# Attention and expert layers on one core: first two attention steps on one side of PSUM, shared steps moved, weight rows loaded a job sooner, warm-up on a cleared tile

## The chip, the cores and the metric

The kernel runs on one core of a Trainium2 chip. The metric is the device time of one execution in microseconds; the median of several runs counts. The engines are named as in the profile: PE is TensorE's matmuls and PEld its weight loads, DVE is VectorE, ACT is ScalarE, POOL is GpSimd, and SP is SyncE, whose queue (SPq) issues nearly all DMA transfers.

## What is computed

An attention with a bias that a small network computes from positions, and on its output a pair of expert matrices with a rational activation between them:

```python
# q, k, v: (4, 8, 576, 64); w1 (1, 32), b1 (32), w2 (32, 8)
scores = q @ k.transpose(0, 1, 3, 2) / sqrt(64)
rel = pos[:, None] - pos[None, :]
x = log1p(abs(rel)) / log1p(maximum(pos[:, None], 1.0))
bias = relu(x[..., None] @ w1 + b1) @ w2          # (576, 576, 8)
attn = softmax(scores + bias.transpose(2, 0, 1))
x = (attn @ v)  -> (2304, 512)
h = x @ w_in                                      # (512, 2048)
g = (a0 + a1*h + a2*h*h + a3*h*h*h) / (1 + abs(b0)*abs(h) + abs(b1)*h*h + 1e-6)
out = g @ w_out                                   # (2048, 512)
```

The weights are split into a high and a low part for the expert matmuls (w_in and w_out arrive in a wider type than the engines work in).

## The kernel before

Three stages follow one another.

**The bias table** (to about 48 us). x depends on the row only by a factor, so the network is evaluated by rows of positions: 36 groups of 16 rows, in the order of the list `order` (groups are counted by their place y in it). For each group four relus go into a ring of 18 slots, on VectorE (line 734) or ScalarE (732); 24 matmul instructions a group (line 761, four column groups of 32) make 128x591 values in two banks of PSUM; ScalarE copies them out into `e` (767); a DMA writes `e` into the table in DRAM (`tab`, line 772); and `load_bias` (260) reads the chunks of the bias back (`bias<-tab`) as they become complete, chunks 3 and 4 of the first pair of heads behind the last group. Ahead of it, nine matmuls (713) on the identity `ident`, which POOL makes, keep TensorE busy for warm-up, and VectorE scales the positions `lts` in two pieces (709). `start(0)` and `start(1)`, which issue the scores and the score reductions of attention steps 0 and 1, stand behind groups y = 33 and 35.

**The attention** (to about 258 us). A unit is a pair of heads, a group two units; a unit's 576 rows are four steps of 128 rows and 64 rows left over. The left-over rows of a group's two units go together in one shared step, `(u, 4)` in the list `steps`; it stands after step `(u, 3)`, so a group has nine steps. Two steps i = 2r and 2r + 1 make a round, `rnd(r)`, r = 1 to 35. A shared step is the first of a round in rounds 3, 11, 20 and 29 and the second in rounds 6, 15, 24 and 33. Each round, in the order of the code: output copies of earlier steps (493), scores of both steps on PE (341) woven together, reduction of scores and bias on VectorE (`e_ttr`, 357), transposes (425) with ScalarE's copies `pt` (440), tails (452), the product with v (484), exponentials on ScalarE (373). `side(i)` says in which four of PSUM's eight banks step i works. `loads`, `done_to` and `load_rb` place the loads of q, k and v, the normalization of a finished unit's output (`e_norm`, line 408, POOL, but VectorE for unit 12 = `NX` and the last unit) and the way of its reciprocals through DRAM (`rs`, 462, and `rb`, 392 and 396) at steps of a group. The list `late` holds unit 12's norm.

Between them `job_plan(r)` lays the preparation of the expert weights: one job for each block, three rounds for two jobs. A job loads raw rows (`wx`, line 140), splits them (VectorE 156 and 181, POOL 177 and 188, ScalarE 165) and stores the high and low part (`ws`, line 128). `out(c)` stores the low part of job c and issues the load of a later job's rows; after round 2 the first loads go out.

**The expert layers** (to the end): lines 316 and 909 on PE, the activation on the others.

Of the kernel before, what the change touches and what calls it, by code (L numbers as in the profile page):

```python
# [9 lines left out]
F32 = mybir.dt.float32  # L10
F32R = mybir.dt.float32r
U32 = mybir.dt.uint32
AF = mybir.ActivationFunctionType
ALU = mybir.AluOpType
# [3 lines left out]
P = 128  # L18
B, H, S, D = 4, 8, 576, 64
# [5 lines left out]
NG = S // NROW  # L25
TW = 2 * S
EW = S + NROW - 1
# [10 lines left out]
def tile_attn_moe(  # L38
# [12 lines left out]
    V, A, G, T = nc.vector, nc.scalar, nc.gpsimd, nc.tensor  # L51
# [4 lines left out]
    ident = cpool.tile([P, P], F32, tag="ident", name="ident")  # L56
# [39 lines left out]
    WF = W.rearrange("p a s -> p (a s)")  # L96
# [136 lines left out]
    with tc.manual_schedule():  # L233
# [3 lines left out]
        with ExitStack() as actx:  # L237
# [68 lines left out]
            def mm1(s, j):  # L306
# [5 lines left out]
                for k in range(KD):  # L312
                    for z, (w, x) in enumerate(
# [4 lines left out]
                            start=(k == 0 and z == 0), stop=(k == KD - 1 and z == 2),  # L318
                        ), b + j)

            steps = [(0, 0), (0, 1), (0, 2), (1, 0), (1, 1), (0, 3), (0, 4), (1, 2), (1, 3)]
            for u in range(2, len(units), 2):
                steps += [(u, c) for c in range(5)] + [(u + 1, c) for c in range(4)]
            s2, prob, pt, tl, xs = {}, {}, {}, {}, {}
            rsum, rb = {}, {}

            def side(i):
                return 4 * ((max(i // 2, 1) - 1 + i) % 2)

            def e_qk(i):  # L330
                u, c = steps[i]
# [177 lines left out]

            def loads(i):  # L510
                g, c = divmod(i, UPG)
                for u, x, y in ((2 * g + 2, 0 if g else 4, 3 if g else 6), (2 * g + 3, 5 if g else 7, 8)):
                    if u < NU and c == x:
                        load_qk(u)
                    if u < NU and c == y and u != 3:
                        load_v(u)
                if i == UPG + 1:
                    load_v(3)
                p, r = divmod(i, 2 * UPG)
                r = {2: 0, 7: 1, 11: 2, 13: 3, 16: 4}.get(r)  # L520
                if r is not None and p + 1 < NP:
                    load_bias(p + 1, r)
                if i == NS - 18:
                    load_x(0, 0, 0, KD - 1)
                if i == NS - 5:
                    load_x(1, 1, 0, KD - 1)
# [3 lines left out]
            def done_to(k):  # L530
                g, c = divmod(k, UPG)
                u = 2 * g - 2
                if g > 0:
                    if c == (0 if g > 1 else 1) and u != NX or k == NS:
                        norms.extend(e_norm(u))
                    if c == 6 and g * 2 < NU:
                        norms.extend(e_norm(u + 1))
                    if c == 2 and u + 1 < NU - 1:
                        load_rb(u + 1)
                if k == NS - 8:  # L540
                    x12.append(xs[NX])
                    late.extend(e_norm(NX))
                if g < NU // 2 and c == (7 - g % 2 if g else 8):
                    load_rb(2 * g)

            def run(todo):
                while todo:
                    todo.pop(0)()
# [11 lines left out]
            def job_plan(r):  # L560
                q, ph = divmod(r - 4, 3)
                c = 2 * q
                plan = {k: [] for k in ("first", "act", "pool", "between", "pool2", "last")}
                if r < 4 or c >= len(jobs):
                    return plan
                a, b = jobs[c], jobs[c + 1]

                def hi(x):
                    return lambda: x[3][3](True, False)

                def out(c):
                    def go():
                        jobs[c][3][3](False, True)
                        run(list(after.get(c, [])))
                        if c + 3 < len(jobs):
                            jobs[c + 3][0]()
                    return go

                if ph == 0:
                    plan.update(first=a[1], act=a[2], pool=[a[4]], last=[a[3][0], hi(a)])  # L580
                elif ph == 1:
                    plan.update(
                        first=b[1], act=b[2], between=[a[3][1]], pool2=[a[3][2]],
                        last=[b[3][0], out(c), hi(b)],
                    )
                else:
                    plan.update(pool=[b[4]], between=[b[3][1]], pool2=[b[3][2]], last=[out(c + 1)])
                return plan

            def rnd(r):  # L590
                i = 2 * r
                plan = job_plan(r)
                loads(i)
                op = None
                while puts:
                    op = puts.pop(0)()
                for x in plan["first"]:
                    op = x()
                for x in plan["act"]:
                    x()  # L600
                us = ended(i - 4, i - 3)
                sa, sb = e_qk(i), e_qk(i + 1)
                b, o = side(i), side(i + 1)
                ZZ = (o + 1, o + 3)
                main, ends, adds, copy = e_tp(i - 2, (b, b + 1), ZZ, us)
                main_, ends_, _, copy_ = e_tp(i - 1, (b + 2, b + 3), ZZ)
                weave(sa[0] + sb[0], sa[1] + sb[1])
                for k in ("pool", "pool2"):
                    if not plan[k] and norms:
                        plan[k].append(norms.pop(0))  # L610
                        break
                for x in plan["pool"]:
                    x = x()
                    if op is not None:
                        behind(x, op)
                e_ttr(i, 0, True)
                op = e_ttr(i, 1)
                for x in plan["between"]:
                    op = x()
                for x in plan["pool2"]:  # L620
                    behind(x(), op)
                small = [ends[r] + ends_[r] + adds[r] for r in range(2)]
                weave(main[0][:4] + small[0] + main[0][4:] + main_[0], main[1] + small[1] + main_[1])
                copy(1, 2)
                copy(0, 1)
                copy_(0, 2)
                for j in range(2):
                    e_ttr(i + 1, j)
                put_tails(i - 2, 2, ZZ, us)
                put = e_pv(i - 3, b + 1) if i > 2 else None  # L630
                puts.append(e_pv(i - 2, b))
                hi = split_x(0, (i - NS + 12) // 2) if i in (NS - 12, NS - 10, NS - 8) else ()
                if i == NS - 4:
                    hi = split_x(0, KD - 1, x12[0][:, :TS[0]])
                for x in hi[:1]:
                    x()
                for k in (i, i + 1):
                    for j in range(2):
                        e_exp(k, j)
                recip(i - 2)  # L640
                recip(i - 1)
                if put:
                    put()
                for x in plan["last"] + list(hi[1:]):
                    x()
                done_to(i - 2)
                done_to(i - 1)
                run(late)
                loads(i + 1)
                if r == 2:  # L650
                    for x in jobs[:3]:
                        x[0]()

            def start(i):
# [33 lines left out]
            with ExitStack() as bctx:  # L688
# [6 lines left out]
                lts = tpool.tile([P, S], F32, tag="lts", name="lts")  # L695
                bts = tpool.tile([P, NG * 4], F32, tag="bts", name="bts")
                LCUT = 320
                nc.scalar.dma_start(out=cs, in_=cst)
                nc.sync.dma_start(out=lts[:, :LCUT], in_=ltab[:, :LCUT])
                nc.sync.dma_start(out=lts[:, LCUT:], in_=ltab[:, LCUT:])  # L700
# [4 lines left out]
                G.memset(wmin, -8.0 * 0x38000000)  # L705
                V.tensor_scalar(out=bts, in0=pts, scalar1=b1s, scalar2=None, op0=ALU.mult)
                A.activation(out=w28, in_=cs[:, 8 + 5 * NG:], func=AF.Identity, scale=8.0)
                for a, z in ((0, LCUT), (LCUT, S)):
                    V.tensor_scalar(
                        out=lts[:, a:z], in0=lts[:, a:z], scalar1=w1s, scalar2=None, op0=ALU.mult  # L710
                    )
                for x in range(9):
                    on(T.matmul(W[:, 6, 0:P], ident, ident, start=True, stop=True), 6)  # L713

                def dist(n):
                    return max(NROW * n + NROW, S - NROW * n)
# [25 lines left out]
                done = {16: 2, 19: 0, 26: 1}  # L742
                for n in order[:LEAD]:
                    relu(n)
                for y, n in enumerate(order):
                    if y == 13:
                        load_v(1)
# [1 line left out]
                        relu(order[y + LEAD])  # L749
                    i0 = NROW * n  # L750
                    mid = i0 + NROW - 1
                    pa = 2 * ((y if y >= NG - 2 else y + 2) % 4)
                    pa = (pa, pa + 1)
                    cuts = sorted({0, mid, 512, EW})
                    for a, z in zip(cuts, cuts[1:]):
# [8 lines left out]
                            ), b)  # L764
                    e = rpool.tile([P, EW], F32, tag="e", name=f"e{n}")
                    o = 512 * pa[0]
                    on(A.activation(  # L767
                        out=e, in_=WF[:, o:o + EW], func=AF.Identity, scale=rts[:, n:n + 1]
                    ), *pa)
                    g, k = divmod(n, 8)  # L770
                    x0 = S - NROW - i0
                    nc.sync.dma_start(
# [307 lines left out]
```

## Time and profile before

| what | value |
|---|---|
| median of 3 runs | 660.83 us (660.64 to 660.9) |
| the profiled execution | 662.25 us, its span 660.5 us |
| granted TensorE clock, mean | 0.999 |
| busy in the span: PE, DVE, ACT, POOL | 99%, 85%, 71%, 23% |
| share of the chain that ended last: PE, DMA, ACT | 96%, 1%, 1% |
| of it by line: 316, 909, 484, 341, 425, 761 | 30%, 30%, 12%, 11%, 6%, 6% |

The profile is one execution; durations are read there, in microseconds from the span's start. Matmuls are pipelined, so PE is busy 99% of the span though parts of it are slower than others: stretches have to be compared with like stretches. The chain that ended last is followed back from the end, and a row in it gives the start, the duration and the number of instructions. A round's length is read as the distance of the rows of line 341 that begin two rounds.

### The profile page before, as it was taken

To read this page: it belongs to the slowest core of one execution; us is meant where nothing else is said; L and a number is where in the kernel's file an instruction comes from. 1 tells how busy PE (TensorE), PEld (TensorE's weight loads), DVE (VectorE), ACT (ScalarE), POOL (GpSimd) and SP (SyncE) were. 2 spreads that over 40 slices of the span, in tenths; PEclk is the share of its full clock that TensorE was granted. 3 is DMA by queue.
4 is the path that set the end of the run, shared out by engine and by line. 5 is a ranking of instruction groups with operands and counts; after the bars stand their busy time and mean duration, and the time that the engine had idled before them with its cause. 6 is when DMAs were issued, how large, how long until landed. Compare 5 with 4: busy or idle time off the path is not lost.

```text
span 660.5 us, 16193 instructions
## 1 busy us (share of the span) xinstructions
PE 653.5 (99%) x6274; PEld 546.8 (83%) x6274; DVE 561.3 (85%) x1100; ACT 472.2 (71%) x758; POOL 154.1 (23%) x108
## 2 busy tenths in 40 slices
PE   9999999999999999999999999999999999999997
PEld 6657888888888878988888888989988888888996
DVE  7997889988988895899999989979769779687776
ACT  7988999999999987767667566576656555555551
POOL 0000233333433330122212121222221221212211
PEclk9999999999999999999999999999999999999999
DMA  7887878868987975452825607669431301312031
GB/s 242 294 310 226 273 240 266 259 228 231 321 277 226 330 238 167 156 187 72 264 97 164 229 21 249 214 207 318 146 111 49 129 0 65 110 42 86 1 113 48
DMA packets 74845, 118.98 MB, mean 180 GB/s; under 512 B 11904, under 2 KB 33808, under 8 KB 74768
## 3 DMA queue, kind: packets, MB, share of 16 engines
q1 hardware_dynamic: 74624, 117.79, 54.2%
q8 instruction: 49, 0.80, 0.5%
q14 instruction: 28, 0.23, 0.1%
q10 hardware_dynamic: 144, 0.16, 0.1%
HBM read 79.17 MB, written 35.61 MB: 174 GB/s over the span
## 4 chain that ended last, share of the span: by engine, by line
PE 96%; DMA 1%; ACT 1%; issue 1%; DVE 0%; SPq 0%; POOL 0%; DVEq 0%; ACTq 0%; POOLq 0%
PE ps L316 30%; PE ps L909 30%; PE ps L484 12%; PE ps L341 11%; PE ps L761 6%; PE ps L425 6%; DMA tab<-e 1%; DMA bias<-tab 1%; PE ps L713 1%; ACT pt L440 1%; ACT p L373 1%; DVE s L357 0%; SPq L260 0%; DVE pre L930 0%; ACT wh L165 0%
## 5 line engine op out<-in xcount | busy, mean ns | idle before, releaser
L879 POOL TENSOR_TENSOR gl<-m,r 128x1024 fp32r<-128x1024 f32 (+1 forms) x39 | 85.6, 2195 | 295.5 <-DVE m L872 255.7
L830 ACT ACTIVATE w<-ps,babs 128x1024 f32<-128x1024 f32 (+1 forms) x40 | 41.3, 1033 | 107.1 <-PE ps L316 103.4
L373 ACT ACTIVATE p<-s,m 128x576 f32<-128x576 f32 x144 | 110.5, 783 | 0.2 <-DVE m L357 0.2
L357 DVE CUSTOM_DVE_ANT_0 s<-ps,bias 128x576 f32<-128x576 f32 (+1 forms) x144 | 95.2, 682 | 10.1 <-PE ps L341 3.9
L440 ACT COPY pt<-ps 128x512 f32<-128x512 f32 (+1 forms) x109 | 71.9, 732 | 17.6 <-PE ps L425 17.0
L909 PE MATMUL ps<-wol,gh 128*128 128x512 f32 x216 | 84.2, 390 | 0.0
L909 PE MATMUL ps<-woh,gh 128*128 128x512 f32 x216 | 84.2, 390 | 0.0
L341 PE MATMUL ps<-k,q 64*128 64x288 f32 (+1 forms) x640 | 82.3, 418 | 0.4 <-ACT e L767 0.2
L842 DVE SCALAR_TENSOR_TENSOR u<-w,babs,ps 128x1024 f32<-128x1024 f32 (+1 forms) x40 | 46.9, 1172 | 38.1 <-ACT t L831 38.0
L484 PE MATMUL ps<-pt,v 128*64 128x128 f32 (+1 forms) x1280 | 78.2, 265 | 0.8 <-ACT pt L440 0.5
L484 PEld LDWEIGHTS ps<-pt,v 128*64 128x64 f32 x1280 | 65.1, 137 | 5.8 <-ACT pt L440 1.6
L316 PE MATMUL ps<-xb,wih 128*128 128x512 f32 (+1 forms) x240 | 68.8, 367 | 0.0
L341 PEld LDWEIGHTS ps<-k,q 64*128 64x128 f32 (+1 forms) x640 | 50.9, 175 | 20.8 <-issue 6.4
L837 ACT ACTIVATE u<-u 128x1024 f32<-128x1024 f32 (+1 forms) x40 | 39.1, 978 | 40.2 <-DVE u L842 40.0
L425 PEld LDWEIGHTS ps<-ident,p 64*128 64x128 f32 x1296 | 49.6, 138 | 8.7 <-DVE m L357 2.9
L858 DVE SCALAR_TENSOR_TENSOR gh<-t,cst,r 128x1024 fp32r<-128x1024 f32 (+1 forms) x40 | 47.0, 1174 | 9.3 <-ACT r L839 6.9
L909 PE MATMUL ps<-woh,gl 128*128 128x512 f32 x216 | 53.8, 389 | 0.0
L425 PE MATMUL ps<-ident,p 64*128 64x64 f32 x1296 | 51.8, 226 | 0.5 <-ACT p L373 0.2
L865 DVE SCALAR_TENSOR_TENSOR m<-u,qc,gh 128x1024 f32<-128x1024 f32 (+1 forms) x40 | 47.1, 1178 | 4.0
L316 PEld LDWEIGHTS ps<-xb,wih 128*128 128x128 f32 x240 | 44.5, 188 | 6.1
L872 DVE SCALAR_TENSOR_TENSOR m<-t,cst,m 128x1024 f32<-128x1024 f32 (+1 forms) x40 | 47.1, 1179 | 1.4
L851 DVE SCALAR_TENSOR_TENSOR t<-t,cst,ps 128x1024 f32<-128x1024 f32 (+1 forms) x40 | 47.0, 1175 | 1.4
(82 smaller groups left out, 1343.9 us busy)
## 6 DMA issues: line engine op xcount, KB each, us to landing
tab<-e SPq DMA_DIRECT2D x36, 295.5 KB, 3.5
wx<-in_w_in_dram SPq DMA_DIRECT2D x16, 512.0 KB, 5.4
wx<-in_w_out_dram SPq DMA_DIRECT2D x16, 512.0 KB, 4.2
v<-in_vp_dram SPq DMA_DIRECT2D x16, 320.0 KB, 6.3
ws<-wh SPq DMA_DIRECT2D x20, 256.0 KB, 4.7
ws<-wl SPq DMA_DIRECT2D x20, 256.0 KB, 4.3
q<-in_qt_dram SPq DMA_DIRECT2D x16, 288.0 KB, 4.1
k<-in_kt_dram SPq DMA_DIRECT2D x16, 288.0 KB, 3.3
```

Of the source, the lines that this page charges most:

```text
L316: on(T.matmul(hps[s][:, j, :w_], w[:, k, sl], x[:, k, :w_], start=(k == 0 and z == 0), stop=(k == KD - 1 and z == 2),), b + j)
L341: on(T.matmul(W[o, b, :SH], q[r, x], k[r, a * SH:(a + 1) * SH], start=True, stop=True), b)
L357: op = on(V.tensor_tensor_reduce(out=t3[:, a], in0=W[:, b:b + 2][:, a, :SH], in1=b3[:, a], scale=-0.125, scalar=least, op0=ALU.add, op1=AL ...
L373: A.activation(out=prob[i][:, z * S:z * S + S], in_=t, func=AF.Exp, bias=m, scale=-1.0, accum_out=sums[u % 4][:, k:k + 1],)
L425: on(T.transpose(W[:, b, o:o + 64], src[x, :], ident[x, x]), b)
L440: on(A.copy(out=t.rearrange("p x (r s) -> p r x s", r=2)[:, a:z], in_=W[:, to[a]:to[a] + z - a].rearrange("p r (x s) -> p r x s", s=64),), ...
L484: on(T.matmul(ps[y, o], vt[n][:, kc, y], w_, start=(kc == 0), stop=(kc == 4)), b, mem=(f"pt{i % 3}", f"tl{i // 2 % 2}"))
L851: on(V.scalar_tensor_tensor(out=rt[s, "t"], in0=rt[s, "t"], scalar=abs_[:, 1:2], in1=hp(s), op0=ALU.add, op1=ALU.mult,), *hb(s), mem="t")
L865: V.scalar_tensor_tensor(out=m, in0=rt[s, "u"], scalar=qc, in1=rt[s, "gh"].bitcast(F32), op0=ALU.add, op1=ALU.mult,)
L872: V.scalar_tensor_tensor(out=m, in0=rt[s, "t"], scalar=abs_[:, 0:1], in1=m, op0=ALU.add, op1=ALU.subtract)
L879: eng.tensor_tensor(out=lo, in0=rt[s, "m"], in1=rt[s, "r0"], op=ALU.mult)
L909: on(T.matmul(po[n, c], l[:, j, c * P:(c + 1) * P], r[fp][:, j, :], start=(first and x is a), stop=(last and x is z),), OB[c])
```

## The change

Five edits, all ahead of the expert layers:

1. `side` puts steps 0 and 1 both into banks 4 to 7 (before: 0 to 3 and 4 to 7); the table groups' banks shift by two groups, and the last group's `e` is made by VectorE instead of ScalarE.
2. `turned` holds groups 1 and 3: their shared step moves one place back, behind step `(u + 1, 0)`, so that it is the first of round 7 and 16. The loads of k, q and v for the next group, `load_rb` and the norms move to fit.
3. `out(c)` loads the rows of job c + 4 instead of c + 3, and ahead of the low part's store; four loads instead of three go out after round 2.
4. `run(late)`, the norm of unit 12, moves from the end of round 33 into round 34, behind the reductions of its first step.
5. The warm-up works on a tile `warm` that VectorE clears, with ten matmuls; the second piece of `lts` is scaled behind the relus of the first two groups.

```diff
+            turned = range(1, len(units) // 2 - 3, 2)
             steps = [(0, 0), (0, 1), (0, 2), (1, 0), (1, 1), (0, 3), (0, 4), (1, 2), (1, 3)]
             for u in range(2, len(units), 2):
-                steps += [(u, c) for c in range(5)] + [(u + 1, c) for c in range(4)]
+                if u // 2 in turned:
+                    steps += [(u, c) for c in range(4)] + [(u + 1, 0), (u, 4)]
+                    steps += [(u + 1, c) for c in range(1, 4)]
+                else:
+                    steps += [(u, c) for c in range(5)] + [(u + 1, c) for c in range(4)]
...
             def side(i):
-                return 4 * ((max(i // 2, 1) - 1 + i) % 2)
+                return 4 * ((i // 2 - 1 + i) % 2) if i > 1 else 4
...
-                for u, x, y in ((2 * g + 2, 0 if g else 4, 3 if g else 6), (2 * g + 3, 5 if g else 7, 8)):
+                for u, x, y in ((2 * g + 2, 0 if g else 4, 3 if g else 6), (2 * g + 3, 7 if g == 0 else 6 if g in turned else 5, 8)):
...
-                    if c == (0 if g > 1 else 1) and u != NX or k == NS:
+                    if c == (1 if g == 1 else 2 if g - 1 in turned else 0) and u != NX or k == NS:
                         norms.extend(e_norm(u))
...
-                if g < NU // 2 and c == (7 - g % 2 if g else 8):
+                if g < NU // 2 and c == (8 if g == 0 else 7 if g in turned else 7 - g % 2):
                     load_rb(2 * g)
...
                     def go():
+                        if c + 4 < len(jobs):
+                            jobs[c + 4][0]()
                         jobs[c][3][3](False, True)
                         run(list(after.get(c, [])))
-                        if c + 3 < len(jobs):
-                            jobs[c + 3][0]()
...
                 op = e_ttr(i, 1)
                 for x in plan["between"]:
                     op = x()
+                run(late)
...
-                run(late)
                 loads(i + 1)
                 if r == 2:
-                    for x in jobs[:3]:
+                    for x in jobs[:4]:
                         x[0]()
...
+                warm = tpool.tile([P, P], F32, tag="warm", name="warm")
+                V.memset(warm, 0.0)
...
-                for a, z in ((0, LCUT), (LCUT, S)):
+
+                def scale(a, z):
...
-                for x in range(9):
-                    on(T.matmul(W[:, 6, 0:P], ident, ident, start=True, stop=True), 6)
+                scale(0, LCUT)
+                for x in range(10):
+                    on(T.matmul(W[:, 6, 0:P], warm, warm, start=True, stop=True), 6)
...
                     relu(n)
+                scale(LCUT, S)
...
-                    pa = 2 * ((y if y >= NG - 2 else y + 2) % 4)
+                    pa = 2 * ((y + 2 if y >= NG - 2 else y) % 4)
...
-                    on(A.activation(
-                        out=e, in_=WF[:, o:o + EW], func=AF.Identity, scale=rts[:, n:n + 1]
-                    ), *pa)
+                    if y < NG - 1:
+                        on(A.activation(
+                            out=e, in_=WF[:, o:o + EW], func=AF.Identity, scale=rts[:, n:n + 1]
+                        ), *pa)
+                    else:
+                        on(V.tensor_scalar(
+                            out=e, in0=WF[:, o:o + EW], scalar1=rts[:, n:n + 1], scalar2=None, op0=ALU.mult
+                        ), *pa)
```

What the tables and positions do to the order on the engines is seen in three places. Line numbers of the changed kernel are some 5 to 16 higher; 341, 357, 408 and 425 become 346, 362, 413 and 430.

PE in rounds 6 and 7 (group 1), before: the shared step's scores (64x288, units 2 and 3 in turn) follow step `(2, 3)`'s in round 6.

```order
L341 MATMUL ps<-k_999,q_998 128x288 x4
L341 MATMUL ps<-k_999,q_998 64x288
L341 MATMUL ps<-k_1204,q_1203 64x288
...
L425 MATMUL ps<-ident,p_1431 128x64 x10
...
L484 MATMUL ps<-tl_1528,v_1102 64x128 x2
L341 MATMUL ps<-k_1204,q_1203 128x288 x8
```

PE in the same rounds now:

```order
L346 MATMUL ps<-k_1002,q_1001 128x288 x4
L346 MATMUL ps<-k_1209,q_1208 128x288 x4
L430 MATMUL ps<-ident,p_1436 128x64 x10
...
L489 MATMUL ps<-tl_1529,v_1107 64x128 x2
L346 MATMUL ps<-k_1002,q_1001 64x288
L346 MATMUL ps<-k_1209,q_1208 64x288
...
L346 MATMUL ps<-k_1209,q_1208 128x288 x4
```

The eight narrow matmuls have gone from the second step of round 6 to the first of round 7, and one step of unit 3 has come forward in their place.

SP's queue between rounds 26 and 28, before (ws are the stores of weight parts, wx the loads of raw rows, rs and rb the reciprocals):

```order
L462 DMA rs_3892<-rt_3891 10x128
L128 DMA ws_0_3807<-wl_0_3839 128x512
L140 DMA wx_1_3937<-in_w_out_dram 128x2048
L128 DMA ws_1_3939<-wh_1_3818 128x512
L392 DMA rb_3941<-rs_3892 64x512
```

and now, at the same place:

```order
L467 DMA rs_3897<-rt_3896 10x128
L140 DMA wx_0_3941<-in_w_in_dram 128x2048
L128 DMA ws_0_3812<-wl_0_3844 128x512
L128 DMA ws_1_3944<-wh_1_3823 128x512
L397 DMA rb_3946<-rs_3897 64x512
```

At one place in the queue the rows of the next block come, where those of this block came, and the store of the low part has gone behind them.

VectorE around the turn from round 33 to 34, before (L408 is the norm of unit 12, L493 the output copies, s_68 and s_69 the reductions of round 34):

```order
L493 COPY xs_4745<-ps 128x128
L408 TENSOR_TENSOR xs_4160<-xs_4160,rb_4532 128x576
L493 COPY xs_4745<-ps 128x128
L357 ISA s_68_0_4785,m_0_0_4786<-ps,bias_2985 128x288
...
L357 ISA m_1_0_4791 128x1
L357 ISA s_69_0_4832,m_0_0_4833<-ps,bias_2985 128x576
```

and now:

```order
L498 COPY xs_4748<-ps 128x128 x2
L362 ISA s_68_0_4786,m_0_0_4787<-ps,bias_2990 128x288
...
L362 ISA m_1_0_4792 128x1
L413 TENSOR_TENSOR xs_4165<-xs_4165,rb_4535 128x576
L362 ISA s_69_0_4835,m_0_0_4836<-ps,bias_2990 128x576
```

The norm has gone from between the two output copies to between the reductions of steps 68 and 69.

## Rows read from the trace of the kernel before

**Rows 1.** page's costly groups: line, engine, operation, count | busy, mean ns | idle

```profile
L909 PE MATMUL ps<-woh,gh 128*128 128x512 f32 x216 | 84.2, 390 | 0.0
```

**Rows 2.** windows, table stage: us, busy of PE, PEld, DVE, ACT, POOL; clock, DMA

```profile
7.67:46.55 38.88, 38.87 (x808) 25.54 (x804) 38.61 (x105) 36.58 (x62) 0.00 (x0) 1.00 0.81 287
```

**Rows 3.** timeline, start: start us, us, engine, line, operation, tiles, count, [idle before <-releaser]

```profile
0.81 0.20 POOL masks.py:197 MEMSET ident<- 128x128 f32 x1
...
1.43 4.21 PE L713 MATMUL ps<-ident 128*128 128x128 f32 x18 [1.43 <-POOL ident masks.py:199]
...
5.57 0.20 PEld L761 LDWEIGHTS ps<-ring,w 128*32 128x32 f32 x8 [0.22 <-ACT ring L732]
5.57 5.86 PE L761 MATMUL ps<-ring,w 128*32 128x271 f32 x112
6.03 0.20 PEld L761 LDWEIGHTS ps<-ring,w 128*32 128x32 f32 x4 [0.26 <-issue]
...
8.83 0.12 PEld L761 LDWEIGHTS ps<-ring,w 128*32 128x32 f32 x4 [0.30 <-issue]
...
9.25 1.32 PEld L761 LDWEIGHTS ps<-ring,w 128*32 128x32 f32 x44 [0.30 <-issue]
```

**Rows 4.** chain of waits, table to attention: start us, us, what, count

```profile
49.74 4.63 DMA tab<-e
55.42 4.37 DMA bias<-tab
...
62.24 2.30 PE ps L341 x24
```

**Rows 5.** waits, 46 to 62.2 us (total, times, longest), and step 1's reduction

```profile
DVE s L357 <- DMA bias<-tab: 1.5, 1, 1.5
...
50.01 0.76 DVE L357 CUSTOM_DVE_ANT_0 s<-ps,bias 128x576 f32<-128x576 f32 x1 [2.10 <-ACT p L373]
```

**Rows 6.** chain of waits, rounds of groups 1 to 4

```profile
79.79 2.30 PE ps L341 x24
...
103.30 2.14 PE ps L341 x16
...
109.10 2.30 PE ps L341 x24
...
114.97 2.14 PE ps L341 x16
...
126.65 2.14 PE ps L341 x16
...
132.44 2.30 PE ps L341 x24
...
179.28 2.14 PE ps L341 x16
```

**Rows 7.** chain of waits, then timeline: round 29

```profile
214.38 1.23 PE ps L341 x16
...
220.70 2.14 PE ps L341 x16
...
211.19 0.41 SPq L140 DMA_DIRECT2D wx<-in_w_out_dram  x1
...
215.38 0.43 DVE L156 TENSOR_SCALAR wk<-wx 128x512 uint32<-128x512 uint32 x1 [0.60 <-DMA wx<-in_w_out_dram]
```

**Rows 8.** chain of waits, timeline of VectorE, waits: rounds 33 and 34

```profile
244.40 0.73 PE ps L341 x4
...
250.54 2.14 PE ps L341 x16
...
240.93 0.69 DVE L181 SCALAR_TENSOR_TENSOR wm<-wm,wh 128x512 uint32<-128x512 uint32 x1
...
244.69 0.76 DVE L408 TENSOR_TENSOR xs<-xs,rb 128x576 f32<-128x576 f32 x1 [0.88 <-DMA rb<-rs]
...
PEld ps L341 <- DVE xs L493: 0.6, 1, 0.6
```

## The prediction, made before the changed kernel was run

> **What bounds the kernel now.** I read the list of costly groups first. The expert layers from 257.7 us on leave TensorE (PE) no idle time [rows 1], so no part of this change, all of which lies ahead of them, can be lost or won there: whatever the attention stage ends earlier shifts the rest of the kernel as a whole. What is to be found is the microseconds ahead of 257.7 us in which PE waits, and whether each of the five edits reaches one.
>
> The windows come next. In the bias-table stage VectorE (DVE) is all but as full as PE: 38.61 of the 38.88 us between 7.67 and 46.55 [rows 2]. A PE that starts sooner there has 0.27 us of DVE's idle time to win, and then meets DVE.
>
> The timeline of the start shows PE's slow stretch. The passes over 271 columns come 0.46 us apart (5.57, 6.03), which is 1.70 ns a column; group 0's passes over 497 columns (its piece from column 15 to 512) come 0.42 us apart (8.83, 9.25), 0.85 ns a column [rows 3]. [...] The passes between them put the rise at about 7.0 us, 5.6 us after the first warm-up matmul at 1.43; behind it the granted clock reads 1.00 [rows 2].
>
> The chain of waits between table and attention shows what sets the start of round 3 (a round is two attention steps, and starts with its scores on line 341): tab<-e, the last table rows going out (49.74, 4.63 us), bias<-tab, their reading back (55.42, 4.37 us), and then the scores at 62.24 [rows 4]. The waits of that stretch say that DVE's score reduction (L357) waits 1.5 us for the bias transfer [rows 5].
>
> Last, the chain through the attention gives each round's length as the distance of two score rows. A plain round is 5.80 us (103.30 to 109.10), one with a shared step in first place 5.87 (109.10 to 114.97) [rows 6]. Two rounds stand out: 214.38 to 220.70 is 6.32 us [rows 7], and 244.40 to 250.54 is 6.14 [rows 8].
>
> **The change, part by part.**
>
> *Warm-up on a cleared tile.* Before, it waits for ident on GpSimd (POOL), whose clearing starts at 0.81 and takes 0.20 us, and a second operation behind it; PE starts at 1.43 [rows 3]. The new tile needs one clearing of the same size, alone on DVE. If DVE begins at about 0.75 as the others do and takes POOL's 0.20, PE starts near 0.98, some 0.45 us sooner. The tenth matmul keeps the end where it was: nine take 4.21 us, ten 4.68, to 5.66, while the first table matmul stands at 5.57 behind the first relus [rows 3], and those still follow the first scaling. If the clock rises as long after the first warm-up as now, it rises 0.45 us sooner, and work done at twice the speed for 0.45 us gains half of that, 0.23. DVE's 0.27 allows it. The second scaling piece, moved behind the first relus, changes DVE's order and not its sum: 0. I take **−0.25**. The ends: 0, if the rise does not move; and −0.7, all that group 0 loses at the slow level (5.57 to 7.0 at half speed), if it rises before the table begins and ScalarE (ACT), which shares the relus, takes what DVE can't.
>
> *Steps 0 and 1 on one side of PSUM, the last eviction on DVE.* Step 1's scores no longer wait for the eviction of a table group but for DVE's reduction of step 0 in the same banks, and the last e stands on DVE between the two. Of the 2.10 us that DVE stands before step 1's reduction at 50.01 [rows 5], the eviction fills about 0.76 (as L408's 576 columns take, [rows 8]) and its wait for PE's last table group a little more; the other half, an estimated 1.0 us, is what rounds 1 and 2 may start sooner. But step 5, the second of round 2, needs a bias chunk that is complete only behind the last table group, and its way (tab out, bias back, 9.0 us of transfers) begins with the last e, which ends when PE's last table group ends, on either engine [rows 4]. So the 1.0 us goes into the wait of 1.5 us for that transfer [rows 5], which becomes 2.5: **0**. The bounds are −1.0, if that transfer comes sooner too, and +0.3, if the eviction ends later on DVE than on ACT by part of its 0.76 us.
>
> *Shared steps of groups 1 and 3 one step later.* A step shared by two units is dearer as the second of a round than as the first. Four rounds with it second, 79.79 to 103.30, take 23.51 us, the next four with it first, 103.30 to 126.65, 23.35: 0.16 less. Group 3's eight rounds, 132.44 to 179.28, take 46.84 as these eight take 46.86, so the same is taken for it [rows 6]. The change makes groups 1 and 3 like 2 and 4. The loads of q, k and v, the reciprocals' way back and two norms on POOL go with it, one step or a round later; POOL is idle most of that stage and the rows that they normalize are read only by the expert layers. **−0.30**; ends 0 (a transfer moved with it comes late) and −0.35.
>
> *Weight loads one job sooner.* Round 29's 0.45 us over a like round (6.32 against 5.87) has its cause in a DVE row: L156 waits 0.60 us for wx, ahead of everything that DVE owes PE in that round; its transfer was issued at 211.19, 3.6 us before it was wanted [rows 7]. With the change this load stands at the place of the one before it, a round earlier or more, so it has landed. Cost: in SP's queue the load now stands ahead of a low-part store, which starts later by one transfer; nothing reads that store for many rounds. One further load of 512 KB goes up front after round 2, where q, k, v and the next bias chunk follow it with several microseconds in hand. **−0.45**; ends 0 (another wait takes its place) and −0.60, DVE's whole wait.
>
> *The norm of unit 12 moved into round 34.* Before, DVE reaches it at the end of round 33 and stands 0.88 us for rb, then 0.76 us on the norm, and only then copies the output (L493) for which PE's weight load waits 0.6 us; that round is 6.14 against 5.80 [rows 8]. After, it stands behind the first step's reductions in round 34; by then rb, there at 244.69, has landed, and the place is where other rounds have the join of L181 (0.69 us) and stay at 5.80 [rows 8]. **−0.35**; ends 0, if DVE is late for step 69's reductions, and −0.40.
>
> *Sum:* −0.25 + 0 − 0.30 − 0.45 − 0.35 = −1.35 us. The profiled execution took 662.25 us, with a span of 660.5; the sum gives it 660.9 and a span of 659.15. The median of the three runs is 660.83, so **659.45** is the forecast, given as 659.4.
>
> **The rivals.**
>
> (a) *The clock rises where it did.* Nothing in the trace shows that the rise follows the first matmul; one rise is there to read. Then the start gives 0, and the time is 660.83 − 1.10 = 659.7. For it: a single reading can't tie the rise to the engine's start. Against: the three runs lie within 0.26 us, and a rise at a random moment would scatter them by up to half of its own scatter.
> [...]
>
> (b) *The start is not held by the bias transfer*, and rounds 1 and 2 bring their 1.0 us: 659.45 − 1.0 = 658.45. For it: the transfer tab<-e of 4.63 us [rows 4] shares the DMA engines with other loads, and may be shorter if those come sooner. Against: the last table rows end with PE, and with DVE full PE's end moves by 0.25 us at most.
>
> (c) *One of the three attention terms comes back*: the norm on DVE in round 34 only moves its 0.76 us in front of step 69, or a load moved with the shared steps is late. Losing one of 0.30 to 0.45, or two in part, gives about 660.0.
>
> (d) *Slower than before: the cleared tile doesn't raise the clock.* Then the rise comes as long after the first table matmul as now after the first warm-up, 5.57 + 5.57 = 11.1 instead of 7.0. Half of those 4.1 us is lost, 2.05, and PE and DVE being both full there, none of it comes back: 660.83 + 2.05 − 1.10 = 661.8. It decides against the change from a rise at 9.2 us on, where half of the delay eats the 1.10. Against it: the engine runs the same instructions on zeros as on ident, and ident is nearly all zeros too.
>
> **How the numbers follow.** Forecast 0.42, (a) 0.24, (b) 0.14, (c) 0.13, (d) 0.07. A measurement of this kernel can tell about 0.2% from no change, 1.32 us: faster is below 659.51, slower above 662.15. The forecast lies at that edge and splits, 0.24 faster and 0.18 same; (a) gives 0.06 and 0.18; (b) is faster; (c) same; (d) 0.02 same and 0.05 slower. That makes 0.44, 0.51 and 0.05. The range: below, 658.4 takes in (b); above, (c) with both small terms lost and no gain at the start ends at about 660.7. Outside are (d) and the tails of (b) and (c), some 0.2. The forecast's own range is 659.0 to 659.9.
>
> **What would show it.** First warm-up matmul near 1.0 us and the pass over 271 columns turning fast before 7.0 (start); L357's wait for bias<-tab growing from 1.5 to 2.5 us with round 3 at 61.9 to 62.1 (no gain by the banks), or staying at 1.5 with round 3 at 61 (b); four-round sums of 23.35 in groups 1 and 3; round 29 at 5.87 and no wait of L156 for wx; round 34 at 5.80 and L408 waiting for nothing. From round 3 to the first expert matmul it should be 1.10 us shorter. A first warm-up later than 1.43, or round 3 after 62.24, makes the start wrong; any round over 5.9 that was 5.8 makes (c) right.

## The result

The changed kernel is slower: 666.81 us against 660.87 for the kernel before, ratio 1.0081 (95% interval 1.0057 to 1.0104). Its six runs spread from 663.22 to 667.49 us, those of the kernel before from 660.51 to 661.89. The forecast was 659.4, with a range from 658.4 to 660.7. The loss is 0.8%, small, but clear of the noise.

The profiled execution took 667.49 us, its span is 665.7 (660.5 before). From the start of each round's scores the place of the loss is found: the changed kernel begins round 28 still 0.25 us ahead of the profile before, then round 28 takes 11.82 us instead of 5.80, and from there to the end it stays 5.2 to 5.8 behind. Here are the chain of waits of the changed kernel around that round (start us, us, what), the waits of ScalarE's and PE's from 204 to 216 us, the row of ScalarE that ends the wait, and the windows (busy us of PE, PEld, DVE, ACT, POOL; then granted clock, DMA share, GB/s):

```profile
207.69 6.58 DMA ws<-wh
...
215.62 4.53 PE ps L489 x40
220.15 2.58 PE ps L346 x24
...
223.90 2.40 PE ps L489 x40
```

```profile
ACT wh L165 <- DMA ws<-wh: 4.1, 1, 4.1
PEld ps L489 <- ACT pt L445: 4.0, 1, 4.0
PE ps L489 <- ACT pt L445: 3.9, 1, 3.9
```

```profile
214.37 0.72 ACT L165 ACTIVATE wh<-wk,wmin 128x512 uint32<-128x512 uint32 x1 [4.07 <-DMA ws<-wh]
```

```profile
206.00:211.50 5.50, 5.50 (x92) 4.85 (x94) 4.71 (x18) 4.30 (x10) 2.62 (x3) 1.00 0.92 256
211.50:215.60 4.10, 0.24 (x8) 0.10 (x4) 1.66 (x8) 1.23 (x3) 0.95 (x1) 0.79 0.76 236
215.60:222.73 7.13, 7.11 (x70) 5.87 (x72) 2.86 (x9) 5.11 (x11) 1.41 (x1) 0.64 0.92 292
222.73:230.00 7.27, 7.21 (x135) 6.30 (x132) 6.52 (x20) 5.96 (x13) 2.70 (x3) 1.00 1.03 381
```

Read from below: ScalarE's line 165 writes the high part `wh` of a weight block. `wh` has two buffers, and the one that it needs is still being stored (`ws<-wh`, issued at 207.69, landed at 214.27). ScalarE stands 4.07 us, and behind it on the same engine stands the copy `pt` (line 445) that PE's product (489) needs. PE is busy 0.24 of 4.10 us, and the granted clock falls to 0.64 as the mean of the next 7 us. The product that takes 2.40 us a round later takes 4.53; over just these 4.53 us the granted clock is 0.50. 3.9 us of waiting and 2.1 us of slow clock make up the 6.0 us of that round.

What answers to the rows of before, in the changed kernel (timeline of the start, waits of 46 to 62.2 us, chain):

```profile
1.05 4.63 PE L723 MATMUL ps<-warm 128*128 128x128 f32 x20 [1.05 <-DVE warm L704]
```

```profile
DVE s L362 <- DMA bias<-tab: 1.9, 1, 1.9
```

```profile
79.58 2.14 PE ps L346 x16
...
102.92 2.14 PE ps L346 x16
...
126.26 2.14 PE ps L346 x16
...
243.96 2.30 PE ps L346 x24
...
249.98 2.14 PE ps L346 x16
...
255.78 2.14 PE ps L346 x16
```

The warm-up starts 0.38 us sooner than in [rows 3]. The wait for the bias transfer grew from 1.5 to 1.9 us [rows 5]. The eight rounds of [rows 6] take 46.68 instead of 46.86, four and four 23.34, so that the first four are 0.17 shorter; the forecast had 0.15 for each group. Round 34 (249.98 to 255.78) takes 5.80 where [rows 8] had 6.14.

### The profile page after: what moved, and what is told of

Its sections match the earlier page's. It is cut to its first block, busy times and chain, and to the rows that moved or that the text cites. A ratio compares the mean times of both kernels' runs of the same rounds, so it can differ in the third digit from the quotient of the medians.

```text
span 665.7 us, 16206 instructions
## 1 busy us (share of the span) xinstructions
PE 655.0 (98%) x6276; PEld 550.2 (83%) x6276; DVE 561.9 (84%) x1102; ACT 470.6 (71%) x757; POOL 153.5 (23%) x108
## 4 chain that ended last, share of the span: by engine, by line
PE 91%; DMA 4%; ACT 2%; SPq 1%; DVE 1%; issue 1%; ACTq 0%; DVEq 0%
PE ps L316 30%; PE ps L925 30%; PE ps L489 11%; PE ps L346 9%; PE ps L772 6%; PE ps L430 5%; DMA ws<-wh 2%; DMA tab<-e 1%; SPq L260 1%; ACT pt L445 1%; DMA wx<-in_w_in_dram 1%; PE ps L723 1%; ACT p L378 1%; DVE s L362 0%; ACT wh L165 0%
## 5 line engine op out<-in xcount | busy, mean ns | idle before, releaser
L489 PE MATMUL ps<-pt,v 128*64 128x128 f32 (+1 forms) x1280 | 80.1, 269 | 5.1 <-ACT pt L445 4.6
L489 PEld LDWEIGHTS ps<-pt,v 128*64 128x64 f32 x1280 | 66.7, 139 | 10.1 <-ACT pt L445 6.6
```

Source lines behind the costliest of these rows:

```text
L489: on(T.matmul(ps[y, o], vt[n][:, kc, y], w_, start=(kc == 0), stop=(kc == 4)), b, mem=(f"pt{i % 3}", f"tl{i // 2 % 2}"))
```

## The experiments

Which part does it? Each run below is compared with the kernel before on the same chip; "ratio" is the ratio of times with its 95% interval.

**1. The changed kernel without the weight loads' edit.** Loads are again those of job c + 3, behind the low part's store, three up front.

> The changed kernel with the weight loads where they were before (job c+3, behind the low part's store, three up front). Theory W (the load ahead of the stores makes the store of a high part land late, and ScalarE's line 165 waits for it): the 4.07 us wait of round 27 goes, PE's clock doesn't fall, and the time is about 660.87 + 6.2 - 0.9 lower than the changed kernel's, 659.9 to 660.4 (round 29 keeps its 0.45). Theory T (the moved shared steps and norm stores make SP's queue late): the wait stays and the time is 664 to 667.

665.58 us, ratio 1.0061 (1.0041 to 1.0082). The waits of ScalarE from 60 to 258 us keep the row:

```profile
ACT wh L165 <- DMA ws<-wh: 2.4, 1, 2.4
```

My first suspicion, the load ahead of the stores (theory W), falls, and with it theory B of the next run, that it takes both edits.

**2. The changed kernel without the moved shared steps.**

> The changed kernel with the shared steps of groups 1 and 3, their loads and norms where they were before. Theory W: the wait of line 165 stays, 664 to 667. Theory T: the wait goes, 659.4 to 660.0. Theory B (it takes both, since each adds a microsecond or two to SP's queue and there was little slack): about 659.8 here and 660.2 without the weight loads' change.

660.57 us, ratio 0.9995 (0.9986 to 1.0004). ScalarE waits for no store. The slowness is gone; the gain that theory T hoped for (659.4 to 660.0) isn't there.

**3. The weight loads' edit alone.**

> The kernel before with only the weight loads a job sooner. Theory W: line 165 waits for a store of a high part by 2 us or more in rounds 25 to 28, 663 to 667. Theories T and B: no such wait over 0.5 us, 660.4 to 661.0.

661.18 us, ratio 1.0008 (0.9999 to 1.0016). Line 165 waits once, 0.7 us in round 29; the profile puts that down to VectorE and not to a store, and what it waited for isn't shown.

**4. The moved shared steps alone.**

> The kernel before with only the shared steps of groups 1 and 3 moved. Theory W and B: 660.87 - 0.3 = 660.5, no wait of line 165 over 0.5 us. Theory T: that wait, 663 to 667.

664.02 us, ratio 1.0046 (1.0027 to 1.0065); the profile has line 165 waiting for stores four times, 3.9 us in all. The shared steps are the cause, alone and in company. With them gone (2, 3) the loss is not there.

**Why.** SP's queue of the changed kernel (start us, us, operation) at the end of group 3, then that of the kernel before at the same place:

```profile
158.54 0.55 SPq L273 DMA_DIRECT2D v<-in_vp_dram  x1
159.14 0.49 SPq L266 DMA_DIRECT2D q<-in_qt_dram  x1
159.68 0.49 SPq L267 DMA_DIRECT2D k<-in_kt_dram  x1
160.27 0.31 SPq L467 DMA_DIRECT2D rs<-rt  x1
160.68 0.34 SPq L140 DMA_DIRECT2D wx<-in_w_out_dram  x1
164.96 0.46 SPq L397 DMA_DIRECT2D rb<-rs  x1
...
169.89 0.65 SPq L196 DMA_DIRECT2D wih<-wh  x1
```

```profile
155.88 0.31 SPq L462 DMA_DIRECT2D rs<-rt  x1
...
158.59 0.55 SPq L392 DMA_DIRECT2D rb<-rs  x1
...
167.04 0.65 SPq L196 DMA_DIRECT2D wih<-wh  x1
...
204.44 0.38 SPq L128 DMA_DIRECT2D ws<-wh  x1
```

and SP's wait in the changed kernel (155 to 167 us):

```profile
SPq L397 <- DMA rs<-rt: 3.9, 1, 3.9
```

With the shared step a round later, the unit's reciprocals (`rs`) are written a round later, but the loads of v, q and k stay, and so come ahead of it. `rb` reads `rs` back and must wait until it has landed: SP stands from 161.0 to 164.96, and everything that is queued behind it is late, the store of `wh` at 167.04 now at 169.89. The lateness shrinks (a store at 180.85 in the profile before goes out at 181.83) and grows again, but it doesn't go away: the store of 204.44 before is the one of 207.69 above. There the buffer had been free in time; now it wasn't. A stand of SP before a read-back is nothing new in itself: between 60 and 200 us the kernel before has five, of 2.4 to 5.0 us (one of them from 195.4 to 198.5), and no wait of line 165. The changed kernel has two besides, 3.6 us from 105.6 on and the 3.9 us above: those of the groups whose shared step was moved.

**5. The moved steps alone, with `rb` one round later still.**

```diff
+                if c == 0 and g - 1 in turned:
+                    load_rb(2 * g - 2)
...
-                if g < NU // 2 and c == (8 if g == 0 else 7 if g in turned else 7 - g % 2):
+                if g < NU // 2 and g not in turned and c == (8 if g == 0 else 7 - g % 2):
```

> The kernel before with the shared steps of groups 1 and 3 moved, and the way back of their reciprocals (rb) one round later still, so that SP reaches rb long after rs has landed. Theory Q (SP stands some 4 us before rb of unit 6, all stores of high parts behind it land late, and ScalarE's line 165 waits for them): no wait of line 165 over 0.5 us between 150 and 230 us, the moved steps' 0.3 us come through, 660.5 to 660.9 beside a before of 660.9 to 661.05. Theory N (the norm's store of unit 6, which has moved beside rs, does it): still 663 to 666.

661.27 us, ratio 0.9999 (0.9986 to 1.0012), no wait of line 165, and SP's two new stands are gone. Theory N falls: the norm's store of unit 6 stands where the change put it. The 0.3 us that the moved steps should bring aren't seen in the time, whose interval is 0.9 us to either side.

**6. The whole change with the edit of 5.**

> The changed kernel whole, with one edit: rb of groups 1 and 3 one round later. Theory Q (SP's stand before rb is what makes the whole change slow): no wait of line 165 over 0.5 us, PE at 2.40 us for every product of round 27 and 28, and 660.5 to 661.6, the time of before. Rival (the weight loads ahead of the stores make a wait of their own once SP is late): 662.5 or more.

661.52 us, ratio 0.9998 (0.9989 to 1.0007). Moving the read-backs of the two groups takes away the whole loss of 0.8%. Its chain at the rounds that were slow:

```profile
205.16 2.40 PE ps L489 x40
207.56 2.14 PE ps L346 x16
209.70 1.26 PE ps L430 x38
210.95 2.40 PE ps L489 x40
```

and its SP queue where the stand was; rs has 5.4 us to land, and the store of `wh` goes ahead of rb:

```profile
155.57 0.31 SPq L467 DMA_DIRECT2D rs<-rt  x1
...
160.30 0.65 SPq L196 DMA_DIRECT2D wih<-wh  x1
161.00 0.64 SPq L397 DMA_DIRECT2D rb<-rs  x1
...
199.83 0.38 SPq L128 DMA_DIRECT2D ws<-wh  x1
```

The last row is the store that went out at 207.69 in the changed kernel.

**7. The moved steps alone, rb where the change has it, but v, q and k behind it.**

> The kernel before with the shared steps of groups 1 and 3 moved as in the change, rb where the change has it, but the loads of v and of the next group's q and k (896 KB) that the change leaves ahead of rs in SP's queue put behind rb, as they stand before. Theory Q1 (rs lands late because those loads are ahead of it in the queues): SP's gap between rs and rb of unit 6 falls from 4.3 us to 3 or less, no wait of line 165 over 0.5 us, about the time of before, 660.5 to 661.3. Theory Q2 (rs itself, a round later, is too late, whatever stands ahead of it): waits of line 165 stay, 663 or more.

663.25 us, ratio 1.0042 (1.0017 to 1.0067). In the profiled execution (span 660.8) `rs` goes out at 157.09 instead of 162.01 in run 4, SP stands 2.7 us before `rb` (157.95 to 160.64; 3.6 in run 4, 0.1 in the kernel before), and line 165 waits only twice, 0.23 and 0.35 us. So the loads ahead of `rs` are a part of the lateness, but with a shorter stand most of the loss in time is still there (1.0042 against 1.0046 in run 4). Neither theory holds whole. The longest round of this profile is round 29 with 6.94 us, where VectorE's L156 waits 1.2 us for `wx`; what the other executions of this kernel waited for, no profile shows.

So the loss hangs on the place of the read-back (5, 6). It leaves why the other four edits, together (6) and in parts (2, 3), bring nothing, where the sum said 1.05 us without the shared steps; the intervals of runs 2 and 6 leave out these 1.05 and the 1.35 of the whole.

**8. The kernel before once more.**

> The kernel before once more, for a second profile. If the profile that the prediction rests on was ordinary, round 3 starts at 62.2 us, round 29 takes 6.33 and round 34 6.14 again. If those waits change from run to run, at least two of the three differ by 0.3 us or more.

661.16 us, ratio to the other runs of the same kernel 1.0007 (0.9997 to 1.0017). Its profiled execution took 660.81, its span 659.0, 1.5 less than the one that I had read. Chain, and VectorE's row for the weights in round 29:

```profile
61.56 2.30 PE ps L341 x24
...
213.70 2.30 PE ps L341 x24
...
219.57 2.18 PE ps L341 x16
...
243.26 2.26 PE ps L341 x16
...
249.11 2.14 PE ps L341 x16
```

```profile
214.01 0.42 DVE L156 TENSOR_SCALAR wk<-wx 128x512 uint32<-128x512 uint32 x1
```

Round 3 begins 0.68 us sooner than in [rows 4], round 29 takes 5.87 instead of 6.32 [rows 7] with no wait for wx, round 34 takes 5.85 instead of 6.14 [rows 8]. These three differences are 0.68 + 0.45 + 0.29 = 1.42 us: all but 0.1 of the distance between the two profiled executions of one kernel.

**9. The start alone (warm-up, one side, last eviction on VectorE).**

> The kernel before with the warm-up on the cleared tile, steps 0 and 1 on one side and the last eviction on VectorE. By the prediction -0.25, 660.7; if round 3 isn't held by the bias transfer -1.0 to -1.2, 659.8; by the first rounds of the traces so far (0.3 to 0.4 us sooner than in kernels without it) 660.5 to 660.7.

661.08 us, ratio 0.9995 (0.998 to 1.001).

**10. The start and the norm in round 34.**

> The kernel before with the start's edits and the norm of unit 12 in round 34 alone. If both terms were worth what one profile showed, -0.25 - 0.35: 660.3 to 660.6. If the start's gain is swallowed by the transfers that round 3 waits for and the norm's wait of the one profile was chance, the time of before, 660.8 to 661.2.

661.26 us, ratio 1.0007 (0.9993 to 1.0022). Both are the time of before. In these two profiles round 4 takes 7.62 and 9.79 us instead of 5.87: L156 waits 1.8 and 2.6 us for `wx`. In the changed kernel and in run 12 the same wait is 0.3 and 0.4 us, in most of the others it isn't there. Which of the two levels PE has at the first table passes of 271 columns is seen in the distance of the weight loads (PEld), here of run 10, whose warm-up begins at 1.05:

```profile
5.61 0.20 PEld L767 LDWEIGHTS ps<-ring,w 128*32 128x32 f32 x8 [0.23 <-ACT ring L737]
6.07 0.20 PEld L767 LDWEIGHTS ps<-ring,w 128*32 128x32 f32 x4 [0.26 <-issue]
```

0.46 us a pass, as in [rows 3], the slow level, though the warm-up began 0.38 us sooner; in the changed kernel the loads of two such passes stand at 5.88 and 6.10, 0.22 us apart. (The granted clock reads 1.00 from 0 to 5 us in the profiles of both kernels; the level is read from the distances alone.) In run 5, which keeps the warm-up of before (1.43), the same passes follow one another in one row of 2.33 us for 64 loads, at the fast level. Over the fourteen profiled executions the first of these passes is slow in five: three of seven with the old warm-up (both of the kernel before, and run 12) and two of seven with the new (1 and 10); in run 3 it takes 0.38 us, between the two.

So the moment moves from execution to execution: with the warm-up of before the passes are fast from 5.44 us on in run 5 and slow until 6.88 in the first profile of the kernel before.

**11. All but the weight loads' edit, with the edit of 5.**

> Start, moved shared steps with rb a round later, and the norm of unit 12 in round 34; weight loads as before. By theory Q -0.35 - 0.3 - 0.35 = -1.0, 659.9 to 660.0. By theory N 663 or more.

661.57 us, ratio 1.0002 (0.999 to 1.0014): no gain either, though the shared steps' rounds and round 34 are as short as forecast in its profile. There is a cost that I had not looked for: round 26 takes 6.19 to 6.24 us in five of the seven profiles with the moved shared steps (the changed kernel, runs 4, 6, 7 and 11), and 5.88 to 5.91 in the other two (1 and 5) and in all seven without them. These 0.3 us are as much as the moved steps bring. In runs 6, 7 and 11 VectorE's first reduction of that round waits 0.44 us for PE's scores; why, no run shows.

**12. The weight loads' edit with the norm of unit 10 cut short.** In runs 2 and 3 rounds 30 and 31 take together 12.72 and 12.56 us, where the kernel before takes 11.73. Run 2 so gives back the 0.45 us of round 29 (5.88 there) and more; run 3 doesn't win them at all, its round 29 takes 6.30, with the wait of line 165 named above. VectorE and GpSimd (POOL) of run 3, then VectorE of run 12:

```profile
218.45 1.42 POOL L408 TENSOR_TENSOR xs<-xs,rb 128x576 f32<-128x576 f32 x1 [6.58 <-DMA rb<-rs]
219.07 1.35 DVE L168 SCALAR_TENSOR_TENSOR wh<-wx,wh 128x512 uint32<-128x512 uint32 x1
219.82 1.73 POOL L188 TENSOR_TENSOR wl<-wm,wh 128x512 fp32r<-128x512 f32 x1
...
226.47 1.04 DVE L156 TENSOR_SCALAR wk<-wx 128x512 uint32<-128x512 uint32 x1
```

```profile
219.06 0.68 DVE L168 SCALAR_TENSOR_TENSOR wh<-wx,wh 128x512 uint32<-128x512 uint32 x1
...
226.02 0.42 DVE L156 TENSOR_SCALAR wk<-wx 128x512 uint32<-128x512 uint32 x1
```

> The kernel before with only the weight loads a job sooner, and unit 10's norm on GpSimd cut to 8 of its 576 columns (the output of that unit isn't normalized). Theory P (the 0.45 us of round 29 are given back because GpSimd, which comes to this norm no sooner, now works beside VectorE's L168, which takes 1.35 instead of 0.72 us, and is late for L181 and beside L156, 1.04 instead of 0.42): L168 and L156 back at 0.72 and 0.42, rounds 28 to 30 shorter by 0.4 to 0.9 than with the loads alone, 660.3 to 660.8. Theory D (the transfers, not GpSimd, slow that round): 661.1 as with the loads alone.

661.94 us, ratio 1.0015 (0.9996 to 1.0035). The time is too scattered (660.6 to 666.63) to tell half a microsecond; the rows do: L168 is back at 0.68, L156 at 0.42, and rounds 30 and 31 are at 5.87 and 5.85. Theory P holds for the rows: VectorE is slow in run 3 beside GpSimd's norm, which waits for `rb` (L168 1.35 us), and beside the next L188 (225.72 to 227.22 there, 223.15 to 224.43 in run 12; L156 1.04 us). That the slow L168 is what lengthens the rounds isn't shown: in run 8 it takes 1.45 us, and rounds 30 and 31 are 5.87 and 5.85 all the same. Nor is a rival told apart: the short norm lets its own store (`xd<-xs`) go out sooner, and the chain of run 3 passes through the landing of that store at 226.30. And it isn't bound to the weight loads: in run 6, with the same edit, these rounds take 5.87 and 5.85, and in run 11, without it, round 31 takes 6.16. That it is worth 0.8 us of the median isn't shown.

In run 3 L168 begins at 219.07, in the norm's time (218.45 to 219.87), and ends at 220.42, 0.55 us after it; why it takes longer there, no run shows.

## Why the prediction was wrong, point by point

- **Shared steps, −0.30.** In the rounds of groups 1 and 3 the term came as forecast, 0.17 and 0.15; round 26 took as much back in most profiles (11). The failed step is its last sentence, "the loads of q, k and v, the reciprocals' way back and two norms on POOL go with it", for which I checked the idle time of POOL and who reads the result, and not SP; the worst that I allowed for a late transfer was that the term becomes 0. The reciprocals' way back contains a wait in SP's queue, and behind it stood the stores that free `wh`. The rule that I had for the weight loads ("nothing reads that store for many rounds") has the same gap, though there no run shows a loss by it: a store may be read by nobody, but it holds the buffer it is read from (`wh`, for which line 165 stood 4.07 us). The loss by this is 5.9 us in the median, and runs 2, 4, 5 and 6 show it. Alone the moved steps cost 3.0 us (4); why they cost more beside the other edits, no run tells apart.
- **Rival (c)** came nearest ("a load moved with the shared steps is late") and priced it at one of the small terms, 0.3 to 0.45. The price was the mistake: this wait held ScalarE (4.07 us), then PE (3.9 us), and then cost the clock (0.50 over the next 4.53 us).
- **Warm-up, −0.25.** Rival (a) is borne out, as far as the runs go: PE starts 0.38 us sooner, the rise isn't seen to follow, and the time of the start's edits alone is 0.9995 of before, though its interval (0.998 to 1.001) is too wide to tell 0.25 us. The profiles tell more: the scores of step 0 begin at 44.34 to 44.80 us in the seven with the old start and at 44.62 to 44.84 in the seven with the new, 44.48 and 44.73 on the mean. The edits of the start and of the banks brought step 0 later, not sooner; which of them, no run shows.
- **Steps on one side, 0.** Right: round 1 begins sooner, at 51.65 us instead of 52.02 on the mean of seven profiles each, and the wait for the bias transfer takes it back: that wait is there in five of the seven with the edit (1.3 to 3.2 us; 1.9 in the changed kernel, where I had 2.5) and in two of the seven without. Round 3 begins at 61.7 and 61.6 on the mean; the 1.0 us of (b) is not there.
- **Weight loads, −0.45, and norm of unit 12, −0.35.** Each was read from one round of one execution. In the second profile of the same kernel both waits were all but gone (8). Without the norm's edit round 34 takes 5.80 to 5.84 in runs 3, 9 and 12, and 6.02 to 6.11 in runs 4, 5 and 7; with it 5.79 or 5.80 in all six profiles. So it removes a wait that appears in about half of the executions. The wait for `wx` in round 29 is there, with 0.3 to 1.2 us, in four of the nine profiles without the loads' edit and in none of the five with it. Neither gain is seen in a median.
- **The base.** The profiled execution took 662.25 us where the median was 660.83. I wrote both numbers down and didn't ask where the 1.42 us lay. They lay in the start and in rounds 29 and 34, and from the last two I had read 0.80 of my 1.35 us: gains read in the longer execution, taken off the shorter median.
- **The sum and the range.** 660.83 − 1.35 is 659.48, not 659.45, and (b) so 658.48; that changes nothing. The upper end as it is described, both small terms and the start lost, is 660.4 and not 660.7. The range reached up by lost gains only. The one slower rival, (d), stood on PE's clock at the start; the clock was lost in round 28 instead.

## What to carry to other kernels

When a step is moved, list for every queue what waits in it and what stands behind that wait; a store behind a read-back keeps a buffer, and the engine that wants the buffer is the one that pays, as ScalarE did here with 4.07 us. A single profiled execution that lies over the median has its surplus somewhere: find those microseconds first, and don't sell them as the gain of an edit. Where PE was the bound and stopped here, its clock cost as well: stops of 1.9, 2.2 and 3.9 us (run 4, run 1, the changed kernel) were followed by a product of 4.07, 4.07 and 4.53 us instead of 2.40, a loss of half to nine tenths of the stop once more.

## What the runs showed of the hardware

- After 3.9 us without work PE ran at a mean granted clock of 0.64 for 7 us; the 40 products took 4.53 us instead of 2.40. After 1.9 us (run 4) and 2.2 us (run 1) they took 4.07.
- The first table pass was slow in five of fourteen profiled executions, with warm-ups that began at 1.05 and at 1.43 us alike (0.45 us a pass at 6.03 in the kernel before, 0.22 us at 5.88 in the changed kernel).
- VectorE's L168 took 1.51 and 1.35 us beside GpSimd's norm (runs 2 and 3) and 0.68 where that norm was cut short (12).
- SP stood 3.9 us before a read-back whose write had gone out behind 896 KB of loads and ahead of 512 KB, and not at all with 5.4 us between the two (run 6).
